# The result's store as two transfers, one for each batch, from the queues of SP and ACT

## Chip, core and metric

One core of a Trainium2 chip runs the whole kernel. The core has five engines with instruction streams of their own: TensorE (PE, with its weight loads shown apart as PEld), VectorE (DVE), ScalarE (ACT), GpSimd (POOL) and SyncE (SP), and 16 DMA engines that all streams share. The metric is the device time in microseconds of one execution, the median over several. A profiled execution also gives a span, from the first to the last instruction of the program; the device time is a little longer than the span.

## The reference

A transformer block for a single new token of two batches (x is 2 x 1 x 512). The conditioning vector c gives six modulation vectors. Attention reads the last 4096 positions of a key and a value cache with 8 heads for 32 query heads, and a feed-forward part of width 1792 follows:

```python
mod = (_silu(c) @ w_mod).reshape(c.shape[0], 6, 1, -1)
sa, ca, ga, sb, cb, gb = (mod[:, 0], mod[:, 1], mod[:, 2], mod[:, 3], mod[:, 4], mod[:, 5])
h = _layernorm(x, axis=-1) * (1 + ca) + sa
x = x + ga * _A_ref(h, A_k_cache, A_v_cache, A_wq, A_wo)
h = _layernorm(x, axis=-1) * (1 + cb) + sb
x = x + gb * _B_ref(h, B_w1, B_w2)
return x
```

`_A_ref` is softmax attention over the window, with the projections wq and wo; `_B_ref` is silu(h @ w1) @ w2. The result has 2 x 1 x 512 numbers, 4 KB, against 97.5 MB of caches and weights that are read.

## The kernel before

All large arrays go through a ring of eight buffers of 128 x 4096 numbers (`ring`, line 55). SP issues every load, one transfer for each buffer, in the order of the program: w_mod, wq, then for each of the eight key heads the keys and values of both batches (`fetch`, line 324), then wo, the small x_sp, and the pieces of w1 and w2 (`load_runs`, line 91). A load into a buffer waits until the work on its last contents is over. So SP's stream is a row of waits and issues, and the engines work on what has landed: DVE turns keys (line 337), PE makes scores and weighted sums (lines 349 and 423), ACT takes exponentials and copies out of PSUM.

A framework gives each transfer one of eight completion semaphores in turn, and a transfer waits for the last one that used the same semaphore before it is issued. In the end a closing block, whose instructions carry the line of the program's end (L680), lets SP wait for the last count of every semaphore; then all engines meet in a handshake.

The end of the kernel is a chain without slack. PE multiplies the hidden vector by w2 (lines 628 to 651): the last pieces w2_11 and w2_13 go into `acc_y` directly, the earlier ones into `acc_yw`, which ACT copies to SBUF (line 522 in `gather`) so that PE can add it. DVE multiplies by gb and adds x1 (lines 653 and 654) to get `yo`. It is a tile of 128 x 128 in which only the rows 0, 16, 32, ... 112 count: row 32g + 16b holds the numbers 128g to 128g + 127 of batch b. `rows8` (line 104) takes these eight rows. One transfer of SP's queue stores them: eight rows of 512 bytes into the 2 x 512 numbers of the result, with the columns' group g outside and the batch b inside:

```python
of = out.rearrange("b s d -> (b s) d")
nc.sync.dma_start(of.rearrange("b (g m) -> g b m", m=P), rows8(yo))
```

ACT issues no transfer in this kernel. Its last work is the copy of line 522.

The small transfers that the store is compared with are those of c_ch and x_ch at the start (line 107: four rows, each of four pieces of 128 bytes, for each batch) and of x_sp (line 474: eight rows of 512 bytes).

Of the kernel before, what the change touches and what calls it, by code (L numbers as in the profile page):

```python
# [13 lines left out]
P = 128  # L14
# [9 lines left out]
def adaln_block(  # L24
# [21 lines left out]
    nc = tc.nc  # L46
# [57 lines left out]
    rows8 = lambda t: t.rearrange("(ab r) m -> ab r m", r=16)[:, 0, :]  # L104
# [58 lines left out]
    for m in range(4):  # L163
        nc.gpsimd.affine_select(
            out=quad,
# [382 lines left out]
    for q in range(24):  # L548
        g = q % 4
# [79 lines left out]
    for tt in range(WIDE):  # L629
        g = tt % 4  # L630
# [21 lines left out]
    yo = once.tile([P, P], F32, tag="yo", name="yo")  # L652
    nc.vector.tensor_mul(yo, y, gb)
    nc.vector.tensor_add(yo, yo, x1)
    of = out.rearrange("b s d -> (b s) d")
    nc.sync.dma_start(of.rearrange("b (g m) -> g b m", m=P), rows8(yo))


_INS = ["A_x", "A_k_cache", "A_v_cache", "A_wq", "A_wo", "B_w1", "B_w2", "c", "w_mod"]
# [24 lines left out]
```

## Time and profile before

| | |
|---|---|
| median of 3 runs | 237.28 us (236.99, 237.28, 237.31) |
| profiled execution | 236.89 us |
| its span | 235.0 us |
| granted TensorE clock, mean | 0.869 of full speed |
| PE busy | 146.5 us, 62% of the span |
| DVE busy | 114.6 us, 49% |
| ACT busy | 25.4 us, 11% |
| bytes moved | 97.69 MB, 416 GB/s on average |

The page gives busy times for each engine, the span in 40 slices with a digit for the busy share in tenths, the DMA queues with their share of the 16 engines' time, and the chain of work that ended last. In other answers of the trace a row names a line of the kernel, an engine, an operation, and out<-in by the names of the program; a name with a small q (SPq, ACTq) is the engine's instruction queue, whose waits and issues of transfers are not counted as busy. The page's share of 62% for PE is the time in which matmuls are in flight, not arithmetic at its peak. What sets the end is read from the chain and from the last stretch of the span.

### The profile page before, as it was taken

To read this page: it belongs to the slowest core of one execution; us is meant where nothing else is said; L and a number is where in the kernel's file an instruction comes from. 1 tells how busy PE (TensorE), PEld (TensorE's weight loads), DVE (VectorE), ACT (ScalarE), POOL (GpSimd) and SP (SyncE) were. 2 spreads that over 40 slices of the span, in tenths; PEclk is the share of its full clock that TensorE was granted. 3 is DMA by queue.
4 is the path that set the end of the run, shared out by engine and by line. 5 is a ranking of instruction groups with operands and counts; after the bars stand their busy time and mean duration, and the time that the engine had idled before them with its cause. 6 is when DMAs were issued, how large, how long until landed. Compare 5 with 4: busy or idle time off the path is not lost.

```text
span 235.0 us, 2644 instructions
## 1 busy us (share of the span) xinstructions
PE 146.5 (62%) x1094; PEld 45.9 (20%) x1094; DVE 114.6 (49%) x176; ACT 25.4 (11%) x56; POOL 10.3 (4%) x30
## 2 busy tenths in 40 slices
PE   0086546367187577667549519626743967788993
PEld 0032101101011121121112102111211222335332
DVE  0634000793694792693892792595298050002130
ACT  2200000100300200200200200200020021003210
POOL 8600000100000000000000000000000000000000
PEclk9999975759869997999976967965985799999999
DMA  6999999999999999999999999999999999999991
GB/s 253 426 438 427 427 438 427 424 439 427 429 441 424 427 438 427 429 438 424 429 435 429 427 432 432 432 429 432 428 429 429 429 432 429 432 426 422 421 412 56
DMA packets 7603, 97.69 MB, mean 416 GB/s; under 512 B 920, under 2 KB 936, under 8 KB 1576
## 3 DMA queue, kind: packets, MB, share of 16 engines
q1 hardware_dynamic: 7592, 97.54, 97.5%
q8 instruction: 8, 0.13, 0.2%
q14 instruction: 3, 0.02, 0.0%
HBM read 97.53 MB, written 0.00 MB: 415 GB/s over the span
## 4 chain that ended last, share of the span: by engine, by line
DMA 64%; DVE 22%; PE 10%; ACT 2%; issue 1%; SPq 1%; DVEq 0%
DVE kT L337 16%; DMA wo<-in_A_wo_dram 14%; DMA k<-in_A_k_cache_dram 14%; DMA v<-in_A_v_cache_dram 13%; DMA wq<-in_A_wq_dram 13%; DMA w<-in_B_w_dram 7%; PE s L349 5%; DMA wm<-in_w_mod_dram 3%; DVE zp L395 2%; PE o L423 2%; PE q L285 1%; DVE xp L393 1%; ACT pr L381 1%; DVE mx L359 1%; ACT L381 1%
## 5 line engine op out<-in xcount | busy, mean ns | idle before, releaser
L337 DVE STREAM_TRANSPOSE kT<-k 128x1024 f32<-128x1024 f32 x64 | 73.7, 1210 | 1.6 <-DMA k<-in_A_k_cache_dram 1.6
L349 PE MATMUL s<-kT,qbd 128*32 128x512 f32 x256 | 44.5, 670 | 11.2 <-DVE kT L337 11.1
L423 PE MATMUL o<-v,ptb 128*32 128x512 f32 x256 | 38.5, 730 | 19.8 <-DMA v<-in_A_v_cache_dram 19.3
L359 DVE TENSOR_REDUCE mx<-s 128x1 f32<-128x512 f32 x8 | 5.5, 691 | 40.1 <-PE s L349 40.1
L349 PEld LDWEIGHTS s<-kT,qbd 128*32 128x32 f32 x256 | 11.1, 126 | 45.8 <-issue 24.1
L285 PE MATMUL q<-wq,hq_T 128*32 128x512 f32 x64 | 11.2, 836 | 10.1 <-DMA wq<-in_A_wq_dram 10.1
L423 PEld LDWEIGHTS o<-v,ptb 128*32 128x32 f32 x256 | 8.1, 124 | 35.8 <-issue 33.1
L402 PE MATMUL pT<-zp,id 128*32 128x256 f32 x64 | 5.6, 418 | 13.9 <-DVE zp L395 13.9
L379 ACT COPY bias<-bp 128x1 f32<-128x1 f32 x8 | 1.3, 159 | 111.9 <-PE bp L377 111.9
L537 PE MATMUL junk<-selh,id 128*32 128x256 f32 x46 | 11.3, 380 | 0.0
L294 DVE STREAM_TRANSPOSE qT<-q 128x512 f32<-128x512 f32 x2 | 1.4, 718 | 18.6 <-PE q L285 18.3
L395 DVE TENSOR_TENSOR zp<-xp,group 128x1024 f32<-128x1024 f32 x8 | 9.8, 1225 | 0.2
L393 DVE STREAM_TRANSPOSE xp<-pr 128x512 f32<-128x512 f32 x8 | 5.6, 701 | 4.4 <-ACT pr L381 4.4
L217 PE MATMUL mean_a<-mv_a,avg 128*128 128x1 f32 x2 | 0.6, 362 | 10.6 <-DVE mv_a L214 10.6
L361 PE MATMUL mT<-ident,mx 128*1 128x128 f32 x16 | 3.0, 270 | 6.4 <-DVE mx L359 6.4
L550 PE MATMUL acc_o<-wo,oTn 128*32 128x512 f32 x48 | 5.8, 598 | 1.9 <-DMA wo<-in_A_wo_dram 1.6
L537 PEld LDWEIGHTS junk<-selh,id 128*32 128x32 f32 x46 | 5.0, 110 | 6.7 <-issue 3.5
L438 PE MATMUL o_all<-ob,selh 128*64 128x128 f32 x64 | 5.7, 304 | 0.8 <-ACT ob L432 0.8
L270 DVE STREAM_TRANSPOSE xT<-x_sp 128x128 f32<-128x128 f32 x1 | 0.4, 403 | 11.8 <-DMA x_sp<-in_A_x_dram 11.8
L432 ACT COPY ob<-o 128x512 f32<-128x512 f32 x8 | 4.7, 585 | 10.3 <-PE o L423 10.3
L285 PEld LDWEIGHTS q<-wq,hq_T 128*32 128x32 f32 x64 | 2.1, 128 | 18.8 <-DMA wq<-in_A_wq_dram 12.5
L249 PE MATMUL m_sp<-wm,scT 128*32 128x512 f32 x32 | 5.7, 796 | 0.0
(132 smaller groups left out, 95.0 us busy)
## 6 DMA issues: line engine op xcount, KB each, us to landing
k<-in_A_k_cache_dram SPq DMA_DIRECT2D x16, 2048.0 KB, 30.2
v<-in_A_v_cache_dram SPq DMA_DIRECT2D x16, 2048.0 KB, 31.5
wq<-in_A_wq_dram SPq DMA_DIRECT2D x4, 2048.0 KB
wo<-in_A_wo_dram SPq DMA_DIRECT2D x4, 2048.0 KB, 32.3
wm<-in_w_mod_dram SPq DMA_DIRECT2D x4, 1536.0 KB, 10.2
w<-in_B_w_dram SPq DMA_DIRECT2D x2, 1024.0 KB, 23.2
w<-in_B_w_dram SPq DMA_DIRECT2D x1, 1792.0 KB
w<-in_B_w_dram SPq DMA_DIRECT2D x2, 896.0 KB
```

The costliest lines, as they stand in the source:

```text
L249: nc.tensor.matmul(m_sp[r, :], scT[:, k, :], cd[:, g], start=(k == 0), stop=(k == 3))
L285: nc.tensor.matmul(q_ps[n][32 * g : 32 * g + 32, :], hq_T[:, k, :], wv[:, n, g], start=(k == 0), stop=(k == 3),)
L337: inorder(nc.vector.transpose(kT[h, b][:, :, 8 * n4 : 8 * n4 + 8, :].rearrange("p j n k -> p n j k"), kt[h, b][:, n4 * 1024 : (n4 + 1) * 1 ...
L349: inorder(nc.tensor.matmul(s_ps[h][r : r + 32, :], qbd[h // 4][:, h % 4, b, j, :], kT[h, b][:, j, 16 * c : 16 * c + 16, :], start=(j == 0) ...
L359: inorder(nc.vector.tensor_reduce(mx, s_ps[h], axis=AX.X, op=ALU.max))
L393: inorder(nc.vector.transpose(xp, pr[h]))
L395: inorder(nc.vector.tensor_mul(zp, xp[:, None, :, 0:16].to_broadcast([P, 4, 16, 16]), group[:, :, None, None].to_broadcast([P, 4, 16, 16]),))
L402: inorder(nc.tensor.matmul(tp[32 * i : 32 * i + 32, :], id4, zp.rearrange("p a s x -> p (a s) x")[:, :, 4 * i : 4 * i + 4], start=True, st ...
L423: inorder(nc.tensor.matmul(o_ps[h][32 * c : 32 * c + 32, :], ptb[h % 2][:, 256 * b + 32 * w : 256 * b + 32 * w + 32], vt[h, b][:, 512 * w ...
L438: inorder(nc.tensor.matmul(o_all[r : r + 64, :], selh[:, m, HQ - G - G * h : 3 * HQ - G - G * h], o_sb[h][:, m * DH : (m + 1) * DH], start ...
L537: inorder(nc.tensor.matmul(junk[0:32, :256], id4, selh.rearrange("p m y -> p (m y)")[:, :256], start=True, stop=True,))
L550: inorder(nc.tensor.matmul(acc[32 * g : 32 * g + 32, :], oTn[:, q, :], wot[q // 8][:, q % 8, :], start=(q < 4), stop=(q >= 20),))
```

## The change

The one store becomes two, written in a loop over the batches: for batch 0 from SP's queue, for batch 1 from ACT's. Each takes every second of the eight rows (32g + 16b for its b) and stores four rows of 512 bytes into the 2 KB of its batch.

```diff
     nc.vector.tensor_mul(yo, y, gb)
     nc.vector.tensor_add(yo, yo, x1)
-    of = out.rearrange("b s d -> (b s) d")
-    nc.sync.dma_start(of.rearrange("b (g m) -> g b m", m=P), rows8(yo))
+
+    for b, queue in enumerate((nc.sync, nc.scalar)):
+        queue.dma_start(out[b, 0, :].rearrange("(g m) -> g m", m=P), rows8(yo)[b : 2 * 4 : 2, :])
```

In the built program ACT's stream gets a wait and a transfer behind the copy of line 522, and SP's keeps a wait and a transfer in the old place. ACT's store takes the completion semaphore that the one store had, SP's the next one. Nothing else changes on any engine: the same instructions stand in the same order. Both queues were set up in the program before, too.

## The prediction

> **What bounds the kernel now.** I read the page's busy slices and queue table first, then the end of the chain of waits, then the stretch behind the last arithmetic, because the change lies there alone.
>
> ```profile
> DMA  6999999999999999999999999999999999999991
> q1 hardware_dynamic: 7592, 97.54, 97.5%
> ```
>
> The loads fill the 16 DMA engines nearly the whole time (97.5% of the span), up to the last slice. Nothing in the change touches a load, so this part stays. What is left is the end. The last pieces of the chain of waits (start, length, what):
>
> ```profile
> 213.97 16.51 DMA w<-in_B_w_dram
> 230.53 1.10 PE acc_y L643 x24
> 231.66 0.30 DVE yo L653
> 231.98 0.29 DVE yo L654
> ```
>
> The last weights arrive at 230.48 us, PE closes acc_y, DVE makes yo in two steps, done at 232.27. The chain as printed stops there; the span of 235.0 does not. The rows of the store's line and of the closing line (L680, the end of the program) show the rest: count, then min/median/max ns, then first and last start.
>
> ```profile
> L656 SPq DMA_DIRECT2D out_dram<-yo x1: 587/587/587, 232.3 to 232.3; - x1
> L656 SPq EVENT_SEMAPHORE  x1: 17/17/17, 218.2 to 218.2; - x1
> L680 SPq EVENT_SEMAPHORE  x8: 17/28/996, 232.9 to 235.0; - x8
> L680 SPq EVENT_SEMAPHORE  x4: 28/28/28, 234.0 to 234.2; - x4
> L680 SPq DRAIN  x2: 7/10/13, 234.3 to 234.3; - x2
> ```
>
> SP issues the store at 232.30 and is busy with it for 0.587 us. At 232.9 it begins the closing waits; the one that starts at 233.0 lasts 0.996 us, that is until the store has landed at 233.99. Four short waits and a drain follow, and a handshake of all engines until 235.03. So the store costs 1.69 us from issue to landing (232.30 to 233.99), then 1.04 us of closing. The packets of the store, in a window of 233.5 to 233.7 us, 40 slices of 5 ns:
>
> ```profile
> DMA  0000400090030039000110300010000000000000
> DMA packets 12, 0.00 MB, mean 21 GB/s; under 512 B 4, under 2 KB 12, under 8 KB 12
> q1 hardware_dynamic: 12, 0.00, 8.9%
> ```
>
> Eight packets of 512 bytes and four short ones (one completion for each engine, so four engines carry the store) take 8.9% of 16 engines x 0.2 us = 0.285 us together, some 0.07 us on each of the four. The data moves between 233.52 and 233.64; the rest of the 1.69 us is the issue, 0.64 us until the first packet and 0.35 us until the landing is seen.
>
> **The change part by part.** The measured execution is 236.89 us around a span of 235.03; the 1.86 us outside are taken as unchanged. It lies 0.39 us below the median of the runs shown, 237.28, to which I add the sum, as the next measurement is also a median.
>
> *SP's store, now four rows.* It keeps its place behind yo and behind an old load's semaphore, which SP's row above shows passing in 17 ns at 218.2. For the issue, the neighbours are these:
>
> ```profile
> L474 SPq DMA_DIRECT2D x_sp<-in_A_x_dram x1: 581/581/581, 181.6 to 181.6; - x1
> L107 SPq DMA_DIRECT2D c_ch<-in_c_dram x2: 532/624/715, 1.2 to 1.9; - x2
> L107 SPq DMA_DIRECT2D x_ch<-in_A_x_dram x2: 522/522/522, 2.5 to 3.1; - x2
> L74 SPq DMA_DIRECT2D wm<-in_w_mod_dram x4: 396/430/448, 0.7 to 4.6; - x4
> L95 SPq DMA_DIRECT2D w<-in_B_w_dram x8: 327/328/328, 184.8 to 216.2; - x8
> ```
>
> Loads over all 128 rows cost SP 0.328 us; those of a few rows 0.52 to 0.59, whatever their number of pieces (x_ch has 16 pieces and takes 0.522, x_sp 8 and 0.581). So half the rows should not halve the issue. I take 0.587 us as before: 0. Lower bound 0.328, a gain of 0.26; upper bound 0.
>
> *The packets.* Two transfers of four 512-byte pieces in place of one of eight: four or eight engines with one or two data packets each and one completion more. By the 0.07 us that an engine spends now, this is between -0.03 and +0.03 us; I take 0.
>
> *ACT's store.* ACT gets two instructions: a wait for an old load's semaphore (17 ns in SP's row, passed long before) and the store. They stand behind its last copy, which starts at 228.62 and takes 0.58 us, so ACT is free from 229.20, 3.1 us before yo. Behind the store is only ACT's drain for the closing handshake; the handshake begins when SP arrives at 234.34, and an ACT issue of 0.6 to 0.85 us from 232.30 is over by 233.15. Some 1.2 us of cover: it costs nothing, unless ACT's issue took over 2 us, and then one for one. Nobody else waits for ACT.
>
> The cost that the trace does not show is ACT's issue itself: ACT issues no DMA in this kernel, so this is its first. The nearest rows are the first ones of SP: its very first load took 396 ns against 328 later (+0.07), its first transfer of few rows 715 ns against 522 to 532 for the next three (+0.19). Both together would be +0.26. Bounds: 0 (ACT issues as a warm SP does) and +0.26 for this alone; I take +0.2, the price of the row that is nearest in kind (a first transfer of few rows).
>
> *The closing waits.* SP still has six, in the same order; the first is now for its own store, the second (where the 0.996 us stood) for ACT's. If ACT's lands last, the chain behind it is the old one: 0. If SP's lands last, one more wait follows it: four waits and two drains between 234.02 and 234.35 make 0.055 us each, so +0.06. I forecast ACT's last, hence 0.
>
> Sum: 0 + 0 + 0.2 + 0 = +0.2 us, 237.1 us against the profiled execution and 237.5 against the median. There is nothing to win on the other side, since before the store there was one issue and after it there are two side by side, none shorter.
>
> **The rivals.**
>
> *The two issues do not run side by side (slower).* SP and ACT both start at 232.30. If what stands behind the issue, the making of the transfer's pieces, serves one queue at a time, the second store comes one issue later. Its price is the pitch at which SP issues two such transfers without a wait between them:
>
> ```profile
> 2.53 1.09 SPq L107 DMA_DIRECT2D x_ch<-in_A_x_dram x2
> ```
>
> 1.09 us for two, 0.55 us each. The second landing is at 234.5, the closing follows unchanged: +0.55, and up to +0.8 with a cold issue of ACT on top: 237.8 to 238.1, 237.9 in the middle. It decides as soon as the second landing is more than 0.47 us (0.2%) behind 233.99; ACT's issue alone, at over 1.06 us, would do the same. For it: the last 1.69 us are bare latency with no other work beside them, so every delay shows in full. Against it: packets of the store occupy four engines for 0.07 us out of 1.69, so the engines are not where two stores would collide, and no row shows two queues at once.
>
> The Trainium skill speaks for this rival: DMA: Bandwidth & Descriptors, section Rules for kernel authors, says that two transfers to disjoint partition halves serialize and that one should be used, and that small transfers should be merged since they are mostly overhead. By that rule the time is this rival's. No run here shows it yet: the trace of before has only one hardware queue with data.
>
> *The halves are cheaper (faster).* If a store whose rows lie alike on both sides (four rows from four pieces) were issued like the plain loads, both issues would take 0.328 us: -0.26, with -0.03 for the packets 237.0. To be faster by 0.47 us it would also have to win 0.18 of the 0.35 us between the last packet and the seen landing, for half the pieces per queue. For it: the store of before has three loops on its far side, the new ones two. Against it: x_sp is as plain, eight rows, and still took 0.581.
>
> **How the numbers follow.** 0.2% of 237.28 is 0.47 us, about what a measurement of this kernel can tell from no change (the three runs lie 0.32 us apart). The forecast, both stores side by side with a cold ACT, gets 0.48: of this 0.35 within 0.2%, 0.13 slower, because +0.2 has a bound of +0.26, a possible +0.06 and the scatter of the medians above it, and ACT is unmeasured. The serial or dear second store gets 0.36: 0.33 slower, 0.03 within, where the two overlap in part. The cheaper halves get 0.16: 0.12 faster, 0.04 within; a part of this is scatter between runs. Together: faster 0.12, within 0.42, slower 0.46. That slower leads though the likeliest single case is a small loss is no contradiction: its size lies near the bound, and the second case adds to it.
>
> The predicted time is 237.5. The likeliest case alone spans 237.1 to 237.8. The range is 236.9 (halves cheaper, 237.0, less 0.1 of scatter) to 238.2 (one pitch of 0.55, +0.26 and +0.06 on top: 238.15).
>
> **What would show it.** Right: SP's store issued at the same distance behind yo, 0.52 to 0.59 us long; ACT's at the same time, 0.7 to 0.85 us; a second hardware queue with eight short and long packets; the two landings 0.1 to 0.3 us apart, ACT's last; everything before 232.3 as it was; the handshake again 1.04 us behind the last landing. Serial: ACT's issue 1.1 us or more, or issues of equal length with the landings 0.5 us apart. Cheaper: an issue of 0.33 us. Wrong altogether: a difference that has arisen before yo, in the loads or on PE, or a shift outside the span.

## The result, and the profile after

| | before | changed |
|---|---|---|
| median | 237.11 us (21 runs, 236.98 to 237.31) | 237.50 us (21 runs, 237.24 to 237.72) |
| profiled execution | 236.89 us, span 235.0 | 237.59 us, span 235.7 |

The ratio of the changed kernel to the one before is 1.0013, 95% interval 1.0007 to 1.0019: 0.31 us slower (0.17 to 0.45); the medians lie 0.39 us apart. This is a real loss, but it lies under the 0.47 us (0.2%) that were set as the bound. The three runs of before that the prediction could see had a median of 237.28; with 21 runs it is 237.11.

The page of the changed kernel shows the second hardware queue, and the loads as they were:

```profile
DMA  7999999999999999999999999999999999999990
...
q1 hardware_dynamic: 7588, 97.54, 97.4%
...
q10 hardware_dynamic: 8, 0.00, 0.0%
```

Four 512-byte pieces have gone from q1 to q10, which is ACT's. Each half has four completions of its own, where the one store had four in all, so q1 loses four packets and q10 has eight. The end in order of time (start, length, engine, line), then the rows of the stores' line and, in windows of 234.2 to 234.4 and 234.69 to 235.02 us, of the closing line (count, min/median/max ns, first and last start):

```profile
232.32 0.29 DVE L654 TENSOR_TENSOR yo<-yo,x 128x128 f32<-128x128 f32 x1
232.64 0.58 SPq L657 DMA_DIRECT2D out_dram<-yo  x1
232.65 1.41 ACTq L657 DMA_DIRECT2D out_dram<-yo  x1
```

```profile
L657 ACTq EVENT_SEMAPHORE  x1: 17/17/17, 229.0 to 229.0; - x1
...
L681 SPq EVENT_SEMAPHORE  x2: 17/156/296, 234.3 to 234.4; - x2
...
L681 SPq EVENT_SEMAPHORE  x4: 28/28/28, 234.7 to 234.9; - x4
L681 SPq DRAIN  x2: 7/10/13, 235.0 to 235.0; - x2
```

Both queues start within 5 ns of each other. SP's issue takes 0.58 us, as before; ACT's takes 1.41 us. SP has its own landing at 234.3 and then waits another 0.296 us, from 234.36 to 234.66, for ACT's. Behind it the four waits, the drains and the handshake are those of before. In a window of 233.8 to 234.4 us (40 slices of 15 ns) the two queues' pieces stand apart:

```profile
DMA  0001020100000000000000000001020100000000
...
q1 hardware_dynamic: 8, 0.00, 1.6%
q10 hardware_dynamic: 8, 0.00, 1.6%
```

SP's pieces move around 233.9, ACT's 0.36 us later. The event times of the traces (the landing of a store is the last update of its completion semaphore), counted from the end of yo, make the comparison finer, since they leave out how early yo was ready in the one execution: before, the store landed at 1.70 us and the program ended at 2.76; changed, SP's half landed at 1.68, ACT's at 2.02, and the program ended at 3.09. That is +0.33 us behind yo, which accounts for the measured 0.31 (0.17 to 0.45). The rest of the 0.7 us between the two profiled spans arose before yo (232.61 against 232.27); the traces of all the kernels here have the end of yo between 232.27 and 232.73, so that is scatter.

### The profile page after: what moved, and what is told of

It is laid out like the page before. It is cut to its first block, busy times and chain, and to the rows that moved or that the text cites. A ratio compares the mean times of both kernels' runs of the same rounds, so it can differ in the third digit from the quotient of the medians.

```text
span 235.7 us, 2646 instructions
## 1 busy us (share of the span) xinstructions
PE 145.9 (62%) x1094; PEld 46.0 (20%) x1094; DVE 114.8 (49%) x176; ACT 25.4 (11%) x56; POOL 10.3 (4%) x30
## 4 chain that ended last, share of the span: by engine, by line
DMA 65%; DVE 19%; PE 11%; ACT 2%; issue 1%; SPq 1%; DVEq 0%
DMA v<-in_A_v_cache_dram 29%; DVE kT L337 14%; DMA wo<-in_A_wo_dram 14%; DMA wq<-in_A_wq_dram 13%; DMA w<-in_B_w_dram 7%; PE s L349 5%; PE o L423 3%; DMA wm<-in_w_mod_dram 3%; DVE zp L395 2%; PE q L285 1%; ACT pr L381 1%; DVE xp L393 1%; DVE mx L359 1%; ACT L381 1%; SPq L74 1%
## 5 line engine op out<-in xcount | busy, mean ns | idle before, releaser
L423 PE MATMUL o<-v,ptb 128*32 128x512 f32 x256 | 39.7, 753 | 23.6 <-DMA v<-in_A_v_cache_dram 23.2
L349 PE MATMUL s<-kT,qbd 128*32 128x512 f32 x256 | 40.6, 626 | 8.3 <-DVE kT L337 8.3
L349 PEld LDWEIGHTS s<-kT,qbd 128*32 128x32 f32 x256 | 10.4, 120 | 40.2 <-issue 22.6
L285 PE MATMUL q<-wq,hq_T 128*32 128x512 f32 x64 | 10.6, 791 | 9.3 <-DMA wq<-in_A_wq_dram 7.4
L550 PE MATMUL acc_o<-wo,oTn 128*32 128x512 f32 x48 | 7.2, 726 | 1.8 <-DMA wo<-in_A_wo_dram 1.4
L377 PE MATMUL bp<-negscale,mrow 1*128 1x1 f32 x16 | 3.0, 256 | 4.2 <-DVE mrow L370 4.2
```

Source lines behind the costliest of these rows:

```text
L285: nc.tensor.matmul(q_ps[n][32 * g : 32 * g + 32, :], hq_T[:, k, :], wv[:, n, g], start=(k == 0), stop=(k == 3),)
L349: inorder(nc.tensor.matmul(s_ps[h][r : r + 32, :], qbd[h // 4][:, h % 4, b, j, :], kT[h, b][:, j, 16 * c : 16 * c + 16, :], start=(j == 0) ...
L423: inorder(nc.tensor.matmul(o_ps[h][32 * c : 32 * c + 32, :], ptb[h % 2][:, 256 * b + 32 * w : 256 * b + 32 * w + 32], vt[h, b][:, 512 * w ...
L550: inorder(nc.tensor.matmul(acc[32 * g : 32 * g + 32, :], oTn[:, q, :], wot[q // 8][:, q % 8, :], start=(q < 4), stop=(q >= 20),))
```

## Experiments

Three theories of ACT's 1.41 us were open: that it is the price of ACT's first transfer (as predicted); that ACT is always that slow; that the two issues get in each other's way. Apart from the one on the closing waits, all edits are to the end of the kernel or add a transfer that nothing reads; "tail" is the time from the end of yo to the end of the program, from the one trace of each kernel.

**One store as before, from ACT alone.**

```diff
-    nc.sync.dma_start(of.rearrange("b (g m) -> g b m", m=P), rows8(yo))
+    nc.scalar.dma_start(of.rearrange("b (g m) -> g b m", m=P), rows8(yo))
```

> The one store of before (eight rows), issued by ACT instead of SP; nothing is issued beside it. Theory 1 (ACT's issue is long, 1.41 us in the changed kernel, because of ACT itself: its first transfer, or its way of issuing): ACT's issue takes 1.3 to 1.5 us again, the landing is seen 2.0 us after the issue begins, and the kernel is 0.3 us slower than before. Theory 2 (the two issues get in each other's way): ACT alone takes 0.55 to 0.65 us, landing after 1.7 us, time as before.

Ratio to before 0.9998 (0.9989 to 1.0007). The row of the store:

```profile
L656 ACTq DMA_DIRECT2D out_dram<-yo x1: 1132/1132/1132, 232.6 to 232.6; - x1
```

Neither theory had this. The issue is long, 1.13 us against SP's 0.59, but the landing comes at 1.78 us instead of 1.70, and the tail is 2.84. The first piece moves at 1.33 us behind yo, only 0.16 us after the issue is shown to end; with SP it is 0.64 us. So much of what is shown as ACT's longer issue lies beside the transfer's own start, and a long issue row is not a late store.

**Both halves from SP.** The loop takes (nc.sync, nc.sync).

> Both half stores from SP, one behind the other. The pitch of SP's small transfers in the profile of before is 0.55 us: the second issue begins 0.57 to 0.63 us after the first, both take 0.52 to 0.59 us, and the kernel is 0.55 to 0.6 us slower than before. If a store of four rows were cheaper for SP once it has just issued one, the second would take 0.33 to 0.4 us and the loss would be 0.35 to 0.4 us.

Ratio 1.0022 (1.0013 to 1.0032), tail 3.39 (+0.63):

```profile
L657 SPq DMA_DIRECT2D out_dram<-yo x2: 523/551/579, 232.5 to 233.1; - x2
```

The second issue follows 0.63 us behind the first and lands 0.58 us later than it (2.25 against 1.67). This is the rival that did not happen: its price was right, and it applies to one queue.

**Both halves from ACT.** The loop takes (nc.scalar, nc.scalar).

> Both half stores from ACT, one behind the other. If ACT's 1.41 us is the price of its first transfer, the first issue takes 1.4 us and the second 0.55 to 0.65 us: 0.9 to 1.0 us slower than before. If every transfer of few rows costs ACT 1.4 us, both take that: 1.7 us slower. If it was contention with SP, both take 0.6 us: 0.6 us slower.

Ratio 1.0046 (1.0029 to 1.0063), tail 3.89 (+1.13):

```profile
L657 ACTq DMA_DIRECT2D out_dram<-yo x2: 515/806/1098, 232.8 to 233.9; - x2
```

The first takes 1.10 us, the second 0.52: ACT is slow only the first time. The first half lands at 1.72 us, 0.04 later than a half from SP alone (1.67, below). The loss is above the 0.9 to 1.0 us that were expected: the second issue starts 1.14 us behind the first and lands 1.04 us behind it (2.75), and 0.08 us are added in the closing waits, as shown below.

**ACT issues a small transfer early.** At the program's start, four rows of 256 bytes, then the changed kernel:

```diff
+    warm = const([P, 64], "warm")
+    nc.scalar.dma_start(
+        rows8(warm)[0 : 2 * 4 : 2, :], x2[0, :256].rearrange("(g m) -> g m", m=64)
+    )
```

> The changed kernel, and ACT issues one more transfer at its start, four rows of 256 bytes of x into a tile that nothing reads. If the 1.41 us is the price of ACT's first transfer, the early one takes 1.3 to 1.5 us and ACT's store then 0.55 to 0.65 us; both stores land together and the time is that of before within 0.1 us. If ACT is always slow, or slow beside SP, its store takes 1.4 us again and the kernel is 0.3 us slower than before.

Ratio 1.0007 (0.9997 to 1.0016), tail 2.93 (+0.17):

```profile
L116 ACTq DMA_DIRECT2D warm<-in_A_x_dram x1: 1105/1105/1105, 0.7 to 0.7; - x1
...
L661 SPq DMA_DIRECT2D out_dram<-yo x1: 579/579/579, 232.5 to 232.5; - x1
L661 ACTq DMA_DIRECT2D out_dram<-yo x1: 567/567/567, 232.5 to 232.5; - x1
```

The price is paid at the start, where it is hidden, and ACT's store is as quick as SP's. Half of the loss in the tail is gone; the interval of the ratio alone would also allow no loss at all. That both land together was not met: ACT's half lands at 1.67 us, as a half alone does (below), SP's now at 1.84. So the other half of the loss is left when both queues have been used and both store at once.

**The changed kernel again.**

> The changed kernel once more, for a second look at its end. If ACT's 1.41 us (against 1.10 to 1.13 us where ACT stores alone) belongs to the two issues meeting, it is 1.35 to 1.45 us again, and ACT's landing again 0.3 to 0.35 us behind SP's. If it was chance, it is 1.1 us and the landing at most 0.1 us behind.

```profile
L657 SPq DMA_DIRECT2D out_dram<-yo x1: 582/582/582, 232.4 to 232.4; - x1
L657 ACTq DMA_DIRECT2D out_dram<-yo x1: 1417/1417/1417, 232.4 to 232.4; - x1
```

1.417 us for ACT's issue, the first piece of ACT again at 1.61 us, landings at 1.67 and 2.03, tail 3.09: the same to 10 ns.

**The one store from ACT, after an early small transfer** (the edits of the first and the fourth experiment together).

> The one store of before (eight rows) from ACT, which has issued one small transfer at its start. If ACT that has issued before is as quick as SP, the issue takes 0.55 to 0.6 us, the program ends 2.76 us behind yo as before, and the time is that of before. If ACT is slower by itself, the issue takes 0.7 us or more and the end comes 0.1 us later.

Ratio 0.9999 (0.9990 to 1.0009):

```profile
L660 ACTq DMA_DIRECT2D out_dram<-yo x1: 612/612/612, 232.7 to 232.7; - x1
```

The issue takes 0.61 us, the landing is at 1.73 us, so ACT that has issued before is as quick as SP to 0.03 us. But the tail is 2.87, 0.11 more. The early transfer has shifted the completion semaphores by one: the store's is now in the first of SP's closing waits, and one more wait follows the landing.

**ACT's half 0.64 us later.** ACT's half is taken from a tile that two more DVE operations make out of yo:

```diff
+    y2 = once.tile([P, P], F32, tag="ax", name="y2")
+    nc.vector.tensor_sub(y2, yo, x1)
+    nc.vector.tensor_add(y2, y2, x1)
-    for b, queue in enumerate((nc.sync, nc.scalar)):
+    for b, (queue, t) in enumerate(((nc.sync, yo), (nc.scalar, y2))):
```

> The changed kernel, but ACT's half is taken from a copy of yo that two more DVE operations make ((yo - x1) + x1), so that ACT's store begins about 0.64 us later, when SP's issue has just ended. If what costs ACT 0.3 us is SP issuing at the same time, ACT's issue is back at 1.1 us and its landing 1.7 us behind its own start. If it is SP's transfer being under way, or nothing of SP's, the issue takes 1.4 us and the landing 2.0 us.

```profile
L660 SPq DMA_DIRECT2D out_dram<-yo x1: 582/582/582, 232.7 to 232.7; - x1
L660 ACTq DMA_DIRECT2D out_dram<-y x1: 1099/1099/1099, 233.3 to 233.3; - x1
```

ACT's first issue, begun 0.07 us after SP's has ended, takes 1.10 us, and its half lands 1.68 us behind its own start. So the last 0.3 us of ACT's 1.41 come from SP issuing at the same time, not from SP's transfer being under way (its pieces move at 1.25 to 1.33 us, inside ACT's issue of 0.68 to 1.78).

**ACT issues a plain transfer over 128 rows early**, then the changed kernel.

```diff
+    warm = const([P, 64], "warm")
+    nc.scalar.dma_start(warm, w_mod[0:P, 0:64])
```

> The changed kernel, and ACT issues one plain transfer over 128 rows at its start, into a tile that nothing reads. If any first transfer pays ACT's price, ACT's store takes 0.57 us, as after the small early transfer. If the price belongs to transfers of few rows apart (SP: first of all 0.40 against 0.33 us, first of few rows 0.72 against 0.53), the early one takes about 0.8 to 0.9 us and the store 0.75 to 0.9 us.

```profile
0.74 0.41 ACTq L116 DMA_DIRECT2D warm<-in_w_mod_dram  x1
...
232.35 0.58 SPq L659 DMA_DIRECT2D out_dram<-yo  x1
232.36 1.42 ACTq L659 DMA_DIRECT2D out_dram<-yo  x1
```

Outside both expectations: the plain transfer costs ACT 0.41 us, what SP's first cost (0.40), and helps the store nothing. The price is that of the first transfer of few rows on ACT. The landings are those of the changed kernel (1.66 and 2.03), but the tail is 3.17 against 3.09, again because ACT's semaphore has moved into the first closing wait.

**The closing waits.** In five kernels (two from SP, two from ACT, one store from ACT used before, ACT's half later, plain transfer first) the tail is 0.08 us longer than the later landing explains: it ends 1.14 us behind the last landing, and 1.06 us behind it before and in the changed kernel. In each of the five the last store's semaphore stands in the first closing wait. So the place of the store's semaphore among the closing waits seems to be worth something. This kernel loads c_ch and x_ch with one transfer each, which moves the one store of before into the last wait:

```diff
     for t, src in ((c_ch, c), (x_ch, x2)):
-        for b in range(B):
-            nc.sync.dma_start(
-                rows8(t)[b : 2 * 4 : 2, :].rearrange("a (k c) -> a k c", k=4),
-                src[b, :].rearrange("(k a c) -> a k c", k=4, a=4),
-            )
+        nc.sync.dma_start(
+            rows8(t).rearrange("r (k c) -> r k c", k=4),
+            src.rearrange("b (k a c) -> a b k c", k=4, a=4),
+        )
```

> A way to a shorter end that the closing waits point to: the one store of before, from SP, with the completion semaphore that SP waits for in the last of its six closing waits instead of the second. Two transfers less in the program do that: c_ch and x_ch are loaded with one transfer each for both batches. The five waits in front are then over while the store is still on its way. If each wait behind the landing costs 0.06 us, four of them go: the program ends 2.50 to 2.55 us behind yo, against 2.76. If the waits are not what takes the time there, it stays 2.76. At the start SP issues two small transfers less (0.55 us each) before the second load of w_mod; if the loads gain from that, yo comes up to 1.1 us earlier, if they are bound by the rate alone, 0 to 0.1 us. Together 0.2 to 1.3 us faster than before.

Ratio to before 0.9988 (0.9979 to 0.9997), 0.28 us faster (0.07 to 0.50). The closing rows, in windows of 232.9 to 233.5 and 234.0 to 234.2 us:

```profile
L679 SPq EVENT_SEMAPHORE  x5: 17/28/28, 233.0 to 233.2; - x5
...
L679 SPq EVENT_SEMAPHORE  x1: 28/28/28, 234.0 to 234.0; - x1
L679 SPq DRAIN  x2: 7/10/13, 234.1 to 234.2; - x2
```

Five waits are now over before the store lands (at 1.70 us, as before), and the sixth is the store's own; the tail is 2.53 instead of 2.76. The loads gain nothing at the start: SP issues the second load of w_mod 1.1 us earlier, yet yo ends at 232.31, inside the scatter. It is the fastest kernel here, with the store in one piece.

**SP's half alone.** The loop takes (nc.sync,) alone.

> SP's half of the changed store alone; the row of batch 1 is left out of the result. It shows what half the pieces save by themselves: the issue 0.58 us, the landing 0.0 to 0.03 us earlier than with eight pieces, the end 2.72 to 2.78 us behind yo (2.76 before).

Landing at 1.67, tail 2.73: half the pieces are worth 0.03 us.

All tails together, in us behind the end of yo:

| kernel | SP's issue | ACT's issue | last landing | tail | ratio to before |
|---|---|---|---|---|---|
| before | 0.59 | | 1.70 | 2.76 | |
| changed | 0.58 | 1.41 | 2.02 | 3.09 | 1.0013 |
| changed, again | 0.58 | 1.42 | 2.03 | 3.09 | |
| one store, ACT | | 1.13 | 1.78 | 2.84 | 0.9998 |
| one store, ACT, used before | | 0.61 | 1.73 | 2.87 | 0.9999 |
| two, SP | 0.58, 0.52 | | 2.25 | 3.39 | 1.0022 |
| two, ACT | | 1.10, 0.52 | 2.75 | 3.89 | 1.0046 |
| changed, ACT used before | 0.58 | 0.57 | 1.84 | 2.93 | 1.0007 |
| changed, ACT 0.64 later | 0.58 | 1.10 | 2.37 | 3.51 | |
| changed, plain transfer first | 0.58 | 1.42 | 2.03 | 3.17 | |
| one store, last wait | 0.59 | | 1.70 | 2.53 | 0.9988 |
| SP's half alone | 0.58 | | 1.67 | 2.73 | |

The differences of the tails (+0.33, +0.08, +0.11, +0.63, +1.13, +0.17, -0.23 us in the rows that were timed) lie inside the intervals of the ratios, so the end of the kernel accounts for each of these times as far as they were measured. The kernels without a ratio were executed once; of them only the trace is used.

## Why the prediction was right, and where it was not

The forecast had the right outcome and nearly the right time: a small loss behind yo, inside 0.2%, with ACT's half landing last. Its chances leaned a little the other way (slower 0.46, within 0.42). But the loss does not come about as the sum has it. The sum puts all of it on ACT's first transfer and nothing on two stores side by side. The runs part the two:

- A first transfer of few rows on ACT, with nothing issued beside it, lands 0.04 us later for a half (1.72 against 1.67) and 0.08 us later for the whole store (1.78 against 1.70).
- Two stores side by side, on queues that have both been used, cost 0.14 us at the later landing (1.84 against 1.70).
- Both together, which is the change, cost 0.33 us (2.02 against 1.70).

So most of the loss is the meeting of ACT's first issue with SP's, which the forecast held to be free. The agreement of 237.5 with 237.50 is luck in part: the sum was +0.2 us on a median of 237.28; measured are +0.39 us between the medians (+0.31 by the ratio) on one of 237.11, and the two misses cancel. Part by part:

- *The loads and all before yo stay, the loss is behind yo.* Right: +0.33 us of tail for +0.31 measured.
- *SP's half costs SP the same issue.* Right: 0.58 against 0.587 us; the lower bound of 0.328 was not approached, and the cheaper halves are refuted (0.03 us for half the pieces).
- *The packets cost nothing.* Right within the bounds of 0.03.
- *ACT is free in time, its drain is covered.* Right. Its issue ends at 234.06, 0.95 us before SP begins the handshake (235.01); of the 1.2 us of cover some was used.
- *ACT's issue: +0.2, bounded by +0.26.* The term that was mis-sized. The later landing came +0.33 us, outside the bounds, and the row of the issue is 1.41 us where 0.7 to 0.85 was expected. The idea, that a first transfer of few rows is dear on ACT as it was on SP, is shown by the second issue of 0.52 us and by the early transfer. But the price was taken from SP's first (0.19 us more), where ACT's row is 0.5 us longer, and it was carried over from the row to the landing one for one, which does not hold: alone, it delays the landing by 0.04 to 0.08 us. Only beside SP's issue does it become +0.33.
- *Two stores side by side cost nothing by themselves.* Wrong: with ACT used before, the later landing still comes 0.14 us behind that of one store, and with ACT's first transfer the meeting costs 0.3 us. This term was missing.
- *The signs.* An issue of ACT of 1.1 us or more was named as a sign of the serial rival, and one of over 1.06 us as enough for a loss of 0.47 us. ACT's issue was 1.41 us and the loss smaller than that. The sign failed because the length of the row is not the delay: from ACT alone a row of 1.13 us, 0.54 us longer than SP's, moved the landing by 0.08.
- *The closing waits: +0.06 if the store's semaphore is an earlier one.* Right in size (0.06 to 0.08 us a wait in the tails, 0.23 for four) and larger in use than the forecast saw: it works in both directions.
- *The serial rival.* Its pitch was right for one queue (0.58 us between the landings). On two queues the landings are 0.18 us apart when both have been used and 0.35 us apart in the changed kernel, so the two stores do delay each other, by about a third and three fifths of that pitch. The Trainium skill, DMA: Bandwidth & Descriptors, section Rules for kernel authors, says that transfers to disjoint partition halves serialize, as both run on the same DMA engines. Here the packets of each half take only 0.15 us of engine time in all (1.6% of 16 engines x 0.6 us), so these runs do not test that reason; the time by the rule, one whole pitch, did not come. Its advice to use one transfer holds: no split of the store was faster than the store in one piece.

Left open: what SP's issue takes away from ACT's first one. At the start of the kernel with the early small transfer ACT's first (0.73 to 1.84 us) lies beside SP's plain load and most of its first c_ch, and takes 1.10 us, so not every overlap with an issue of few rows costs it the 0.3. And in the kernel with the plain transfer first, ACT's and SP's plain issues begin 10 ns apart and take 0.41 and 0.39 us, where SP's alone takes 0.40. Whenever both issue their half at once, one half lands as if it were alone (1.66 to 1.68 us) and the other one later. A step that serves one queue at a time would do that, but no run isolates one: in the changed kernel the delay of ACT's half is there before its first piece (1.61 us, against 1.28 where both halves come from ACT), while with ACT used before only half of the delay of SP's is (first piece at 1.33 against 1.24, landing at 1.84 against 1.67).

## What to carry to other kernels

At the end of a kernel nothing hides a transfer's latency, and a store of a few KB is issue and round trip, not bytes: splitting it buys the 0.03 us of its pieces and can cost ten times that. An engine whose queue has not yet issued a transfer of that kind should not make its first one on the critical path, above all beside another queue's; if a second queue must store, let it issue a small one early, which took away half of the loss here. And look at what the program waits for behind the store: the same store was worth 0.23 us more or less by the place of its semaphore in the closing waits.

## What was not expected of the hardware

- ACT's first transfer of few rows takes 1.10 to 1.13 us of its queue, later ones 0.52 to 0.61; a plain one over 128 rows before it (0.41 us) does not change that. SP's first of few rows takes 0.70 to 0.73, later ones 0.52 to 0.60.
- The length of an issue row is not the delay of its transfer: 1.13 us in place of 0.59 moved the landing by 0.08 us.
- The same first issue beside SP's is 1.41 to 1.42 us in three traces of two kernels, and then the landing does move, by 0.33 us.
- The end of the changed kernel repeats to about 10 ns between its two traces (tails of 3.09 us), while the time to yo scatters by some 0.4 us; a change of 0.1% at the end is read more safely from the tail than from the total.
